# Load order, V of the first tiles, eviction engines and a split last tile in a gated attention and feed-forward kernel

## The chip, the cores and the metric

The kernel runs on one core of a Trainium2 chip. The metric is the device time of one execution in microseconds (us), measured over several executions. The profile's "span", from the first to the last instruction, is about 2 us shorter than that time. Engines are named as in the profile: PE (TensorE matmul), PEld (its weight loads), DVE (VectorE), ACT (ScalarE), POOL (GpSimd), SP (SyncE, which only issues DMA here).

On a single core "slow" cannot mean that one die is slower than the other. It means a run over 1.5% above the fastest of its kernel.

## The reference

```python
x = A_x                                              # 2048 x 512, bf16
g = sigmoid((x * gate_w).sum(-1))
# A: linear attention, 32 heads of 16
q, k, v = split(x @ wqkv)
pq, pk  = q @ w_phi[h], k @ w_phi[h]                 # per head, 16 x 16
phi     = concat(softmax(p), softmax(-p))            # for q and k
num, den = phi_q @ (phi_k^T v),  phi_q @ sum(phi_k)
a = (num / den) @ wo
# B: two-layer perceptron, 1376 hidden
b = relu(x @ w1) @ w2
out = g * a + (1 - g) * b
```

## The kernel before

The program is one list of operations per engine; each waits for named events. PE's order is what matters most. It multiplies `x` by W1 in "units" (`hunit`: 4 matmuls of 128x512, then a Relu on ScalarE); there are 4 column groups of 512 rows of x, with 11 units each. It folds `w_phi` into the Q and K weights (`pre`), which needs those weights transposed; then it runs 16 attention tiles of 128 rows (`atile`), with the units of groups 1 and 2 between them, then the units of group 3, then 16 output tiles.

The loads, in their order of issue (cuts marked `...`):

```python
for j in range(4):                     # x rows 0..511, two tiles each on SP's and ScalarE's queue
    p.dma(("sp", "act")[j // 2], ... out=XS[:, j, :], in_=x2[...], ev=f"x0{j}")
w1cuts = [0, 256, 512, 1024, DFF]      # four pieces of W1 on ScalarE's and SP's queues
for i in range(4):
    p.dma(("act", "act", "sp", "sp")[i], ... out=W1[:, :, a:b], ... ev=f"w1{i}")
p.dma("pool", ... out=WPS ...)         # w_phi, then four tiny loads of gate_w
...
p.wait("pool", ["x01", "x03"])
p.wait("sp", ["x03"])
p.dma("pool", ... out=WV ...)                                    # V's weight, 512 KB
p.dma("sp", ... dma_start_transpose(out=WQKT, in_=A_wqkv[:, 0:2 * D]))   # Q and K weights, 1 MB
for c in range(1, NCH):                                          # x rows 512..2047, transposed
    p.dma("sp", ... dma_start_transpose(out=XT[...], in_=x2[...]))
```

One attention tile. Q and K share one pair of PSUM banks, so that the matmuls of tile m + 1 wait for the last Exp of tile m (`em`):

```python
def atile(m):
    first = xready(m // 4) + [f"em{m - 1}"]
    ...  # PE: 8 matmuls, Q and K, into banks 0 and 1
    ...  # PE: 4 matmuls, V, into bank 2, after the V copy of tile m - 1
    ...  # ScalarE: Exp(+) and Exp(-) of both banks, 128x1024 each: ep, em
    p.op("dve", ... tensor_copy(VS[:, b, :, 0:64], PS[:, 2, :] ...), ev=f"cv{m}")       # V copy
    p.op("dve", ... tensor_reduce(ZB[:, b, 64:128], ...), after=[f"em{m}"])             # sums for K
    p.op("dve", ... reciprocal(SC[:, b, 64:128], ...))
    p.op("dve", ... tensor_reduce(ZB[:, b, 0:64], ...))                                 # sums for Q
    p.op("dve", ... reciprocal(SC[:, b, 32:64], ...))
    p.op("dve", ... tensor_tensor(SC[:, b, 0:32], ..., ALU.mult), ev=f"sc{m}")          # small product
    p.op("pool", ... K scaled ...);  p.op("pool", ... Q scaled ...)
    p.dma("sp", ... dma_start_transpose(out=PHQ[...], in_=FM[:, b, 0, :]))
```

The order on PE:

```python
for kt in range(8): hunit(0, kt)
pre()                                     # needs the transposed Q and K weights
for kt in range(8, KT): hunit(0, kt)
for m in range(NT):
    atile(m)
    want = (m + 1) * len(mid) // NT       # 22 units over 16 tiles
    while done < want: hunit(*mid[done]); done += 1
    if m >= LAG: kv(m - LAG)
...  # late units, kvfin(), gate(), finB(0), nd(0), nd(1), finB(1), nd(2), finA(0), comb(0), finA(1), comb(1)
for m in range(2, NT):
    if m + 1 < NT: nd(m + 1)              # PHI of Q times KV; VectorE divides, DMA transposes to OT
    finB(m); finA(m); comb(m)             # W2 product, WO product (ScalarE scales), VectorE combines
```

The softmax here doesn't subtract the row's maximum and nothing guards it: scores larger than these inputs give would overflow.

## Time and profile before

Three timed runs took 168.22 to 170.77 us, median 168.73. The profile shown first is of a slow execution (172.73 us, span 170.9).

From the page of the kernel before: busy tenths of the engines, the granted PE clock and the DMA rate in 40 slices of 4.3 us each.

```profile
PE   6469369999999999989999999897999999999991
DVE  3500032199999999999999994155453355434531
PEclk9969956999999999999999999999999999999999
GB/s 137 259 155 104 150 225 166 186 267 62 61 61 65 63 61 63 61 47 80 61 61 61 37 89 61 1 31 83 74 84 69 88 69 63 92 67 90 61 83 40
```

Up to slice 7 PE has gaps and a low clock; from slice 9 to 24 VectorE is at 9; after that PE alone is full. The gaps of the start are named by the chain of waits (start us, length us, what):

```profile
4.83 18.19 DMA PHQ<-in_A_wqkv_dram
...
23.06 3.59 PE PS L253 x32
26.65 3.67 PE PS L223 x12
30.32 1.74 PE PS L273 x8
```

The transposing load of the Q and K weights (`PHQ` lends its space) takes 18.2 us, then come the products of `pre` (L253), three units (L223) and the first QK tile (L273). While that load is under way, the DMA rate collapses. The stretches are of the same profile; their last number is GB/s, the one before the DMA share, and before that stands the clock:

```profile
4.00:8.00 4.00, 1.84 (x18) 1.18 (x16) 2.16 (x8) 0.00 (x0) 1.25 (x2) 1.00 0.90 244
12.00:16.00 4.00, 2.90 (x14) 1.37 (x15) 0.00 (x0) 1.46 (x4) 0.00 (x0) 1.00 1.25 88
16.00:20.00 4.00, 2.45 (x12) 0.90 (x10) 0.00 (x0) 2.29 (x4) 0.00 (x0) 1.00 1.18 94
22.00:26.00 4.00, 2.94 (x28) 2.94 (x29) 1.97 (x3) 1.36 (x3) 0.00 (x0) 0.50 1.18 234
```

Plain loads alone (4 to 8 us) move 244 GB/s, transposes alone (22 to 26 us) 234, the two together about 90, with the DMA engines shown as busy throughout.

A stretch of the tiles shows what VectorE (the third busy time, 42.96 of 44 us) is doing there:

```profile
38.00:82.00 44.00, 43.05 (x256) 20.26 (x256) 42.96 (x61) 28.01 (x36) 30.14 (x21) 1.00 0.32 61
```

| stage (span of the slow profile) | us | what fills it |
|---|---|---|
| start to the first QK tile | 0 to 30.2 | weight load; PE at half clock after waiting |
| tiles, first QK to last QK | 30.2 to 93.4 | 4.22 us per tile on PE; VectorE 98% busy |
| last tile and late units | 93.4 to 109.4 | PE |
| output | 109.4 to 170.9 | PE, 3.5 us per tile |

### The profile page before, as it was taken

Reading aid. Unit: us, or ns where it says so; the run is one execution under the profiler, and the core shown is the slowest. Engines: PE = TensorE matmul, PEld = TensorE weight load, DVE = VectorE, ACT = ScalarE, POOL = GpSimd, SP = SyncE. Lnnn points to the kernel's source line nnn. Section 1 sums busy time; section 2 is a strip of 40 time slices with the busy share of each in tenths; the row PEclk is TensorE's granted clock in tenths of the full one; section 3 lists DMA queues with packets and bytes.
Section 4 is the critical chain, followed back from the end, with each engine's and each line's share of the span. In section 5 each row is a group of like instructions: output and inputs, shape, how many; then the busy total and the mean of one; then the engine's idle time right before and its main releaser. Section 6 shows DMA issues by size and latency. Waiting matters only on the chain.

```text
span 170.9 us, 2373 instructions
## 1 busy us (share of the span) xinstructions
PE 153.3 (90%) x919; PEld 73.3 (43%) x919; DVE 104.2 (61%) x174; ACT 73.3 (43%) x102; POOL 54.6 (32%) x48
## 2 busy tenths in 40 slices
PE   6469369999999999989999999897999999999991
PEld 2314065434444445444434454353445544454440
DVE  3500032199999999999999994155453355434531
ACT  3024325886657577575566666403111311122111
POOL 8200000456666666666666664000000000000000
PEclk9969956999999999999999999999999999999999
DMA  4999998672225222253222332013232332324231
GB/s 137 259 155 104 150 225 166 186 267 62 61 61 65 63 61 63 61 47 80 61 61 61 37 89 61 1 31 83 74 84 69 88 69 63 92 67 90 61 83 40
DMA packets 42378, 15.57 MB, mean 91 GB/s; under 512 B 37136, under 2 KB 41760, under 8 KB 42368
## 3 DMA queue, kind: packets, MB, share of 16 engines
q1 hardware_dynamic: 40192, 12.17, 37.3%
q0 software_dynamic: 832, 2.48, 4.9%
q10 hardware_dynamic: 1344, 0.79, 1.7%
q8 instruction: 7, 0.11, 0.3%
q14 instruction: 3, 0.02, 0.0%
HBM read 4.41 MB, written 2.10 MB: 38 GB/s over the span
## 4 chain that ended last, share of the span: by engine, by line
PE 44%; DVE 32%; DMA 14%; issue 6%; ACT 2%; ACTq 0%; DVEq 0%
PE PS L384 21%; DMA PHQ<-in_A_wqkv_dram 11%; DVE ZB L294 9%; DVE ZB L299 9%; PE PS L223 9%; PE PS L394 8%; DVE VS L291 5%; DVE SC L302 3%; DMA OT<-in_A_x_dram 2%; PE PS L253 2%; PE PS L360 2%; DVE SC L297 2%; DVE SC L304 2%; DMA OT<-OTM 1%; ACT FM L288 1%
## 5 line engine op out<-in xcount | busy, mean ns | idle before, releaser
L223 PE MATMUL PS<-XT,W 128*128 128x512 bf16 (+1 forms) x176 | 44.3, 397 | 3.8 <-DVE Wbd L200 2.2
L384 PE MATMUL PS<-W,HT 128*128 128x512 bf16 (+1 forms) x176 | 40.6, 379 | 0.9 <-ACT EG L347 0.8
L288 ACT ACTIVATE FM<-PS 128x1024 bf16<-128x1024 f32 x32 | 31.0, 1021 | 20.6 <-PE PS L273 20.6
L307 POOL TENSOR_TENSOR FM<-FM,SC 128x1024 bf16<-128x1024 bf16 x16 | 30.8, 1927 | 22.9 <-DVE SC L297 22.9
L237 ACT ACTIVATE HT<-PS 128x512 bf16<-128x512 f32 (+1 forms) x44 | 26.2, 598 | 16.9 <-PE PS L223 16.8
L399 ACT ACTIVATE TFA<-PS,GT 128x512 bf16<-128x512 f32 x16 | 11.0, 687 | 47.5 <-PE PS L394 47.5
L223 PEld LDWEIGHTS PS<-XT,W 128*128 128x128 bf16 (+1 forms) x176 | 17.9, 104 | 25.5 <-issue 2.9
L405 DVE SCALAR_TENSOR_TENSOR OSB<-PS,OMG,TFA 128x512 bf16<-128x512 f32 x16 | 12.0, 751 | 27.6 <-ACT TFA L399 27.6
L273 PE MATMUL PS<-WqP,XT 128*128 128x512 bf16 x64 | 24.3, 380 | 1.0 <-ACT FM L288 0.6
L273 PE MATMUL PS<-WkP,XT 128*128 128x512 bf16 x64 | 24.2, 379 | 0.0
L384 PEld LDWEIGHTS PS<-W,HT 128*128 128x128 bf16 (+1 forms) x176 | 16.2, 97 | 18.7 <-issue 1.2
L294 DVE TENSOR_REDUCE ZB<-FM 128x64 f32<-128x1024 bf16 x16 | 19.3, 1204 | 0.4 <-ACT FM L288 0.4
L299 DVE TENSOR_REDUCE ZB<-FM 128x64 f32<-128x1024 bf16 x16 | 18.6, 1161 | 0.0
L311 POOL TENSOR_TENSOR FM<-FM,SC 128x512 bf16<-128x512 bf16 x16 | 16.9, 1055 | 2.0
L279 PE MATMUL PS<-WV,XT 128*128 128x512 bf16 x64 | 16.5, 380 | 1.1 <-DVE VS L291 0.9
L394 PE MATMUL PS<-WO,OT 128*128 128x512 bf16 x64 | 16.4, 378 | 1.0 <-DMA OT<-OTM 1.0
L291 DVE CAST VS<-PS 128x512 bf16<-128x512 f32 x16 | 10.9, 679 | 6.0 <-PE PS L279 6.0
L370 DVE TENSOR_TENSOR OTM<-PS,RDEN 128x512 bf16<-128x512 f32 x16 | 11.1, 692 | 0.5
L258 DVE CAST WqP<-PS 128x512 bf16<-128x512 f32 x2 | 1.4, 691 | 15.6 <-PE PS L253 15.6
L279 PEld LDWEIGHTS PS<-WV,XT 128*128 128x128 bf16 x64 | 5.8, 98 | 10.0 <-DVE VS L291 3.8
L273 PEld LDWEIGHTS PS<-WqP,XT 128*128 128x128 bf16 x64 | 6.2, 97 | 8.6 <-ACT FM L288 2.5
L394 PEld LDWEIGHTS PS<-WO,OT 128*128 128x128 bf16 x64 | 6.1, 97 | 8.8 <-issue 0.9
(48 smaller groups left out, 94.7 us busy)
## 6 DMA issues: line engine op xcount, KB each, us to landing
out_dram<-OSB SPq DMA_DIRECT2D x16, 128.0 KB, 1.7
W<-in_B_w_dram POOLq DMA_DIRECT2D x1, 1280.0 KB, 6.6
W<-in_B_w_dram ACTq DMA_DIRECT2D x2, 256.0 KB, 8.6
W<-in_B_w_dram SPq DMA_DIRECT2D x1, 512.0 KB, 6.9
WV<-in_A_wqkv_dram POOLq DMA_DIRECT2D x1, 512.0 KB, 14.6
WO<-in_A_wo_dram POOLq DMA_DIRECT2D x1, 512.0 KB, 6.8
W<-in_B_w_dram SPq DMA_DIRECT2D x1, 352.0 KB, 10.8
OT<-in_A_x_dram ACTq DMA_DIRECT2D x2, 128.0 KB, 3.0
```

The costliest lines, as they stand in the source:

```text
L223: p.op("pe", lambda e, c=c, kt=kt, M=M, dt=dt, bank=bank: e.matmul(PS[0:M, bank, :], W1[:, dt, kt * P:kt * P + M], XT[:, dt, c * 512:(c + ...
L237: p.op("act", lambda e, c=c, kt=kt, Mr=Mr, bank=bank: e.activation(HT[0:Mr, kt, c * 512:(c + 1) * 512], PS[0:Mr, bank, :], ACT.Relu), afte ...
L273: p.op("pe", lambda e, m=m, dt=dt, which=which, W=W: e.matmul(PS[:, which, :], XT[:, dt, m * P:(m + 1) * P], W[:, dt, :], start=(dt == 0), ...
L279: p.op("pe", lambda e, m=m, dt=dt: e.matmul(PS[:, 2, :], XT[:, dt, m * P:(m + 1) * P], WV[:, dt, :], start=(dt == 0), stop=(dt == NDT - 1) ...
L288: p.op("act", lambda e, o=fm5[:, :, :, s, :], i=src, s=s: e.activation(o, i, ACT.Exp, scale=(1.0 if s == 0 else -1.0)), after=[f"qk{m}"] + ...
L291: p.op("dve", lambda e, b=b: e.tensor_copy(VS[:, b, :, 0:64], PS[:, 2, :].rearrange("p (g c) -> p g c", g=NG)), after=[f"v{m}"] + ([f"kv{m ...
L294: p.op("dve", lambda e, b=b: e.tensor_reduce(ZB[:, b, 64:128], FM[:, b, 1, :].rearrange("p (g f) -> p g f", f=DH), AX.X, ALU.add), after=[ ...
L299: p.op("dve", lambda e, b=b: e.tensor_reduce(ZB[:, b, 0:64], FM[:, b, 0, :].rearrange("p (g f) -> p g f", f=DH), AX.X, ALU.add), ev=f"zq{m}")
L307: p.op("pool", lambda e, b=b, fk=fk: e.tensor_tensor(fk, fk, SC[:, b, 64:128].unsqueeze(2).to_broadcast([P, 2 * H, DH]), ALU.mult), after= ...
L311: p.op("pool", lambda e, b=b, fq=fq: e.tensor_tensor(fq, fq, SC[:, b, 0:32].unsqueeze(2).to_broadcast([P, H, DH]), ALU.mult), after=[f"sc{ ...
L384: p.op("pe", lambda e, kt=kt, M=M, m=m, bank=bank: e.matmul(PS[:, bank, :], HT[0:M, kt, m * P:(m + 1) * P], W2[0:M, kt, :], start=(kt == 0 ...
L394: p.op("pe", lambda e, t=t, m=m, bank=bank: e.matmul(PS[:, bank, :], OT[:, t, m * P:(m + 1) * P], WO[:, t, :], start=(t == 0), stop=(t == ...
```

## The change

Its intent: no transposing transfer overlaps a plain one; PE does V of the first tiles where it used to wait for the weights (the "filler"); VectorE is relieved of the V copy (to ScalarE) and of the small product (to GpSimd); the last output tile is cut in two halves so that its evictions overlap matmuls. The diff, cut to its core:

```diff
+        w1cuts = [0, 384, 896, DFF]
+        for j in range(4): p.dma("sp", ... out=XS[:, j, :] ...)      # x, all on SP's queue
+        load_w1(0) ... load_w1(1); load_w1(2)                        # W1 now on GpSimd's queue
+        p.dma("pool", ... out=WV ...);  p.dma("pool", ... out=WPS ...)
         for dt in range(NDT):
-            p.dma("pool", ... W1[:, dt, DFF:DFF + 1], in_=gate_w ...)
+            p.dma("sp", ... W1[:, dt, DFF:DFF + 1], in_=gate_w ...)
-        p.wait("pool", ["x01", "x03"])
-        p.wait("sp", ["x03"])
+        p.wait("sp", ["w12", "wv"])
         p.dma("sp", ... dma_start_transpose(out=WQKT ...))
...
-                p.dma("sp", ... out=GL ...)                          # gate logits
+                p.dma("act", ... out=GL ...)
...      # atile: V matmuls and V copy move out, into vtile(m)
-            p.op("dve", ... tensor_tensor(SC[:, b, 0:32] ...), ev=f"sc{m}")
+            p.op("pool", ... tensor_tensor(SC[:, b, 0:32] ...), ev=f"sc{m}")
+        def vtile(m): ...            # V copy: VectorE for m < 4, ScalarE for the others
...
-        for kt in range(8): hunit(0, kt)
-        pre()
-        for kt in range(8, KT): hunit(0, kt)
+        for kt in range(KT): hunit(0, kt)
+        vtile(0); vtile(1); pre(0); vtile(2); pre(1); vtile(3)
         for m in range(NT):
             atile(m)
-            want = (m + 1) * len(mid) // NT
+            if m >= 4: vtile(m)
+            want = 2 * (m + 1) if m < 4 else 8 + (m - 3) * (len(mid) - 8) // (NT - 4)
...
+        last(NT - 1)     # W2 product of columns 0..255, WO product, W2 product of columns 256..511
```

Not shown: ScalarE takes two of the four copies of x's transposes out of PSUM, and VectorE builds its masks after the other two instead of before them.

More of the change, by code (lines that the diff above doesn't have):

```diff
@@ L133, in bass_gated_mix__linear_kernel_hedgehog__dense_activation_relu__prompt_kernel, with load_w1 @@
         p = _Plan(["sp", "pool", "act", "dve", "pe"])
+        w1cuts = [0, 384, 896, DFF]
+        def load_w1(i):
+            a, b = w1cuts[i], w1cuts[i + 1]
+            p.dma("pool", lambda e, a=a, b=b: e.dma_start(
+                out=W1[:, :, a:b], in_=B_w1[:, a:b].rearrange("(j p) n -> p j n", p=P)), f"w1{i}", ev=f"w1{i}")
         p.op("dve", lambda e: e.memset(WARM[:, :], 1.0), ev="warm")
+        for j in range(4):
+            p.dma("sp", lambda e, j=j: e.dma_start(out=XS[:, j, :], in_=x2[j * P:(j + 1) * P, :]),
+                  f"x0{j}", ev=f"x0{j}")
+        load_w1(0)
         p.op("pool", lambda e: e.iota(COLI[:, :], [[1, P]], channel_multiplier=0))
         p.op("pool", lambda e: e.iota(ROWI[:, :], [[0, P]], channel_multiplier=1), ev="iota0")
+        load_w1(1)
+        load_w1(2)
+        p.dma("pool", lambda e: e.dma_start(
+            out=WV[:, :, :], in_=A_wqkv[:, 2 * D:3 * D].rearrange("(j p) n -> p j n", p=P)), "wv", ev="wv")
+        p.dma("pool", lambda e: e.dma_start(
+            out=WPS[:, :, :], in_=A_w_phi.rearrange("(g hl) r c -> (hl r) g c", g=NDT)), "wps", ev="wps")
         p.op("pool", lambda e: e.iota(COL16[:, :], [[1, 8], [0, 16]], channel_multiplier=0), ev="iota1")
@@ L141, in bass_gated_mix__linear_kernel_hedgehog__dense_activation_relu__prompt_kernel @@
              after=["iota0"], ev="idn")
-        p.op("dve", lambda e: e.tensor_single_scalar(ROW16[:, :], ROWI[:, :], 4, ALU.arith_shift_right), ev="r16")
-        p.op("dve", lambda e: e.tensor_single_scalar(ROW32[:, :], ROWI[:, :], 5, ALU.arith_shift_right), ev="r32")
-        p.op("dve", lambda e: e.tensor_tensor(M16[:, :], ROW16[:, :], COL16[:, :], ALU.is_equal),
-             after=["iota1", "r16"], ev="m16")
-        p.op("dve", lambda e: e.tensor_tensor(M32[:, :], ROW32[:, 0:64], COL16[:, 0:64], ALU.is_equal),
-             after=["r32"], ev="m32")
-        for b in range(NB):
-            p.op("dve", lambda e, b=b: e.memset(VS[:, b, :, 64:65], 1.0), ev=f"one{b}")
-        for j in range(4):
-            p.dma(("sp", "act")[j // 2], lambda e, j=j: e.dma_start(out=XS[:, j, :], in_=x2[j * P:(j + 1) * P, :]),
-                  f"x0{j}", ev=f"x0{j}")
-        w1cuts = [0, 256, 512, 1024, DFF]
-        for i in range(4):
-            a, b = w1cuts[i], w1cuts[i + 1]
-            p.dma(("act", "act", "sp", "sp")[i], lambda e, a=a, b=b: e.dma_start(
-                out=W1[:, :, a:b], in_=B_w1[:, a:b].rearrange("(j p) n -> p j n", p=P)), f"w1{i}", ev=f"w1{i}")
-        p.dma("pool", lambda e: e.dma_start(
-            out=WPS[:, :, :], in_=A_w_phi.rearrange("(g hl) r c -> (hl r) g c", g=NDT)), "wps", ev="wps")
         for dt in range(NDT):
-            p.dma("pool", lambda e, dt=dt: e.dma_start(
+            p.dma("sp", lambda e, dt=dt: e.dma_start(
                 out=W1[:, dt, DFF:DFF + 1], in_=gate_w[dt * P:(dt + 1) * P].rearrange("(p o) -> p o", o=1)),
                 "gw", ev=f"gw{dt}")
-        p.wait("pool", ["x01", "x03"])
-        p.wait("sp", ["x03"])
-        p.dma("pool", lambda e: e.dma_start(
-            out=WV[:, :, :], in_=A_wqkv[:, 2 * D:3 * D].rearrange("(j p) n -> p j n", p=P)), "wv", ev="wv")
+        p.wait("sp", ["w12", "wv"])
         p.dma("sp", lambda e: e.dma_start_transpose(out=WQKT, in_=A_wqkv[:, 0:2 * D]), "wqk", ev="wqk")
@@ L196, in bass_gated_mix__linear_kernel_hedgehog__dense_activation_relu__prompt_kernel @@
             dst = XT[:, :, j * P:(j + 1) * P]
-            p.op("dve", lambda e, s=src, d=dst: e.tensor_copy(d, s), after=[f"xt{j}"], ev=f"xc{j}")
+            if j % 2 == 0:
+                p.op("dve", lambda e, s=src, d=dst: e.tensor_copy(d, s), after=[f"xt{j}"], ev=f"xc{j}")
+            else:
+                p.op("act", lambda e, s=src, d=dst: e.activation(d, s, ACT.Copy), after=[f"xt{j}"], ev=f"xc{j}")
+        p.op("dve", lambda e: e.tensor_single_scalar(ROW16[:, :], ROWI[:, :], 4, ALU.arith_shift_right), ev="r16")
+        p.op("dve", lambda e: e.tensor_single_scalar(ROW32[:, :], ROWI[:, :], 5, ALU.arith_shift_right), ev="r32")
+        p.op("dve", lambda e: e.tensor_tensor(M16[:, :], ROW16[:, :], COL16[:, :], ALU.is_equal),
+             after=["iota1", "r16"], ev="m16")
+        p.op("dve", lambda e: e.tensor_tensor(M32[:, :], ROW32[:, 0:64], COL16[:, 0:64], ALU.is_equal),
+             after=["r32"], ev="m32")
+        for b in range(NB):
+            p.op("dve", lambda e, b=b: e.memset(VS[:, b, :, 64:65], 1.0), ev=f"one{b}")
         for gt in range(NDT):
@@ L215, in hunit @@
             M = P if kt < KT - 1 else KREM + 1
-            w1s = [i for i in range(4) if w1cuts[i] <= kt * P < w1cuts[i + 1]][0]
+            w1s = [i for i in range(3) if w1cuts[i] <= kt * P < w1cuts[i + 1]][0]
             after = xready(c) + [f"w1{w1s}"]
@@ L232, in hunit @@
                     after=[f"h{u}"], ev=f"gr{c}")
-                p.dma("sp", lambda e, c=c: e.dma_start(
+                p.dma("act", lambda e, c=c: e.dma_start(
                     out=GL[:, c * 4:(c + 1) * 4],
@@ L239, in hunit, with pre @@
                 after=[f"h{u}"], ev=f"rl{u}")
-        def pre():
-            PB = [0, 1, 2, 6, 7]
-            for i in range(8):
+        def pre(half):
+            PB = [0, 1, 6, 7]
+            for i in range(4 * half, 4 * half + 4):
                 which, dt = i // 4, i % 4
-                bank = PB[i % 5]
+                bank = PB[i % 4]
                 dst = (WqP, WkP)[which]
                 after = ["wqk"] + [f"wbd{g}" for g in range(NDT)]
-                if i < 4:
-                    after.append(f"xc{i}")
-                if i >= 5:
-                    after.append(f"pc{i - 5}")
+                if i == 0:
+                    after.append("cv1")
+                if i >= 4:
+                    after.append(f"pc{i - 4}")
                 for gt in range(NDT):
@@ L277, in atile @@
                         ev=(f"qk{m}" if dt == NDT - 1 and which == 1 else None))
-            for dt in range(NDT):
-                p.op("pe", lambda e, m=m, dt=dt: e.matmul(
-                    PS[:, 2, :], XT[:, dt, m * P:(m + 1) * P], WV[:, dt, :],
-                    start=(dt == 0), stop=(dt == NDT - 1)),
-                    after=((["wv"] + ([f"cv{m - 1}"] if m else [])) if dt == 0 else ()),
-                    ev=(f"v{m}" if dt == NDT - 1 else None))
             fm5 = FM[:, b, :, :].rearrange("p a (h s f) -> p a h s f", h=H, s=2)
@@ L290, in atile @@
                     after=[f"qk{m}"] + free, ev=f"{nm}{m}")
-            p.op("dve", lambda e, b=b: e.tensor_copy(
-                VS[:, b, :, 0:64], PS[:, 2, :].rearrange("p (g c) -> p g c", g=NG)),
-                after=[f"v{m}"] + ([f"kv{m - NB}"] if m >= NB else []), ev=f"cv{m}")
             p.op("dve", lambda e, b=b: e.tensor_reduce(
@@ L299, in atile @@
             p.op("dve", lambda e, b=b: e.tensor_reduce(
-                ZB[:, b, 0:64], FM[:, b, 0, :].rearrange("p (g f) -> p g f", f=DH), AX.X, ALU.add), ev=f"zq{m}")
+                ZB[:, b, 0:64], FM[:, b, 0, :].rearrange("p (g f) -> p g f", f=DH), AX.X, ALU.add),
+                after=([f"sc{m - NB}"] if m >= NB else []), ev=f"zq{m}")
             zq = ZB[:, b, 0:64].rearrange("p (h s) -> p h s", s=2)
             p.op("dve", lambda e, b=b, zq=zq: e.reciprocal(SC[:, b, 32:64], zq[:, :, 1]),
-                 after=[f"zq{m}"] + ([f"pq{m - NB}"] if m >= NB else []), ev=f"rq{m}")
-            p.op("dve", lambda e, b=b, zq=zq: e.tensor_tensor(SC[:, b, 0:32], zq[:, :, 0], SC[:, b, 32:64], ALU.mult),
-                 after=[f"rq{m}"], ev=f"sc{m}")
+                 after=[f"zq{m}"] + ([f"sc{m - NB}"] if m >= NB else []), ev=f"rq{m}")
             fk = FM[:, b, 1, :].rearrange("p (g f) -> p g f", f=DH)
@@ L309, in atile @@
                 after=[f"rz{m}"], ev=f"pk{m}")
+            p.op("pool", lambda e, b=b, zq=zq: e.tensor_tensor(SC[:, b, 0:32], zq[:, :, 0], SC[:, b, 32:64], ALU.mult),
+                 after=[f"rq{m}"], ev=f"sc{m}")
             fq = FM[:, b, 0, :].rearrange("p (h s f) -> p h s f", h=H, s=2)[:, :, 1, :]
@@ L316, in atile, with vtile @@
                 f"tq{b}", after=[f"pq{m}"] + ([f"pm7"] if m == 12 else []), ev=f"tq{m}")
+        def vtile(m):
+            b = m % NB
+            bank = 0 if m == 1 else 2
+            prev = {0: [], 1: [], 2: ["cv0"]}.get(m, [f"cv{m - 1}"])
+            for dt in range(NDT):
+                p.op("pe", lambda e, m=m, dt=dt, bank=bank: e.matmul(
+                    PS[:, bank, :], XT[:, dt, m * P:(m + 1) * P], WV[:, dt, :],
+                    start=(dt == 0), stop=(dt == NDT - 1)),
+                    after=((xready(m // 4) + ["wv"] + prev) if dt == 0 else ()),
+                    ev=(f"v{m}" if dt == NDT - 1 else None))
+            dst, src = VS[:, b, :, 0:64], PS[:, bank, :].rearrange("p (g c) -> p g c", g=NG)
+            after = [f"v{m}"] + ([f"kv{m - NB}"] if m >= NB else [])
+            if m < 4:
+                p.op("dve", lambda e, d=dst, s=src: e.tensor_copy(d, s), after=after, ev=f"cv{m}")
+            else:
+                p.op("act", lambda e, d=dst, s=src: e.activation(d, s, ACT.Copy), after=after, ev=f"cv{m}")
         def kv(m):
@@ L410, in comb, with last @@
                 out=o2[m * P:(m + 1) * P, :], in_=OSB[:, ob, :]), f"out{ob}", after=[f"cb{m}"], ev=f"out{m}")
-        for kt in range(8):
-            hunit(0, kt)
-        pre()
-        for kt in range(8, KT):
-            hunit(0, kt)
+        def last(m):
+            ob = m % 3
+            for hf in range(2):
+                if hf == 1:
+                    finA(m)
+                bank = (5 - m % 2, 0)[hf]
+                cs = slice(hf * 256, hf * 256 + 256)
+                after = [f"cb{m - 2}", f"om{m - 1}"]
+                for kt in range(KT):
+                    M = P if kt < KT - 1 else KREM
+                    p.op("pe", lambda e, kt=kt, M=M, bank=bank, cs=cs: e.matmul(
+                        PS[:, bank, 0:256], HT[0:M, kt, m * P:(m + 1) * P], W2[0:M, kt, cs],
+                        start=(kt == 0), stop=(kt == KT - 1)),
+                        after=(after if kt == 0 else ()), ev=(f"fb{m}{hf}" if kt == KT - 1 else None))
+            for hf in range(2):
+                bank = (5 - m % 2, 0)[hf]
+                cs = slice(hf * 256, hf * 256 + 256)
+                p.op("dve", lambda e, bank=bank, cs=cs: e.scalar_tensor_tensor(
+                    out=OSB[:, ob, cs], in0=PS[:, bank, 0:256], scalar=OMG[:, m:m + 1],
+                    in1=TFA[:, m % 2, cs], op0=ALU.mult, op1=ALU.add),
+                    after=[f"fb{m}{hf}", f"ta{m}", f"out{m - 3}"], ev=f"cb{m}{hf}")
+                p.dma("sp", lambda e, cs=cs: e.dma_start(
+                    out=o2[m * P:(m + 1) * P, cs], in_=OSB[:, ob, cs]), f"last{hf}",
+                    after=[f"cb{m}{hf}"], ev=f"last{hf}")
+        for kt in range(KT):
+            hunit(0, kt)
+        vtile(0)
+        vtile(1)
+        pre(0)
+        vtile(2)
+        pre(1)
+        vtile(3)
         mid = [(c, kt) for c in (1, 2) for kt in [KT - 1] + list(range(KT - 1))]
@@ L422, in bass_gated_mix__linear_kernel_hedgehog__dense_activation_relu__prompt_kernel @@
             atile(m)
-            want = (m + 1) * len(mid) // NT
+            if m >= 4:
+                vtile(m)
+            want = 2 * (m + 1) if m < 4 else 8 + (m - 3) * (len(mid) - 8) // (NT - 4)
             while done < want:
@@ L444, in bass_gated_mix__linear_kernel_hedgehog__dense_activation_relu__prompt_kernel @@
         comb(1)
-        for m in range(2, NT):
-            if m + 1 < NT:
-                nd(m + 1)
+        for m in range(2, NT - 1):
+            nd(m + 1)
             finB(m)
@@ L450, in bass_gated_mix__linear_kernel_hedgehog__dense_activation_relu__prompt_kernel @@
             comb(m)
-        p.wait("sp", [f"out{m}" for m in range(NT - 3, NT)])
+        last(NT - 1)
+        p.wait("sp", [f"out{m}" for m in range(NT - 3, NT - 1)] + ["last0", "last1"])
         sems = {}
```

## The prediction

> **What bounds the kernel now** (timeline, chain of waits, windows).
>
> 1. Start, 0 to 30.2 us. The transposing load of the Q and K weights is issued at 4.83 us and lands 18.2 us later, while plain loads of W1 and V's weight share the DMA engines. In 12 to 20 us the DMA moved only 63 to 113 GB/s, against 240 to 260 for plain loads alone (2 to 8 us) and 220 to 264 for transposes alone (20 to 28 us). PE runs 8 of the 11 first units, waits 4.6 us for the weights, and comes back at half clock (granted 0.50 from 22 to 28 us). The first QK tile starts at 30.15.
> 2. Sixteen tiles, to 98.4 us. VectorE's work comes back every 4.37 us (V copy 0.68, reductions 1.20 and 1.16, reciprocals 0.55 and 0.35, product 0.55), 98% busy. PE needs about 4.0 us per tile (a 128x512 matmul every 0.2155 us).
> 3. Eleven late units, to 109.4 us, PE bound.
> 4. Sixteen output tiles at 3.5 us, PE bound, and a tail: ScalarE 0.69, VectorE 0.75, store about 2.
>
> **What the change does.**
>
> Start: plain loads first. 2.43 MB at about 255 GB/s is 9.5 us, landed by about 12 us. Then the transposing load of 1 MB runs alone: 2.4 us of issue per 0.5 MB (as the x transposes) plus 2 us to land, so it lands at about 19. Meanwhile PE has all 11 units and V of two tiles (13 x 0.86 us from about 6.5 us, plus up to 1.7 while the clock is low), so it arrives at 18 to 19.5, with almost no wait, and warm. The Trainium skill ("TensorE: Matmul & The Clock Gate", Part 1) says idleness of about 3.4 us halves the clock; the 0.50 after the 4.6 us wait agrees. With weight products, eight evictions (0.69 VectorE, 0.60 ScalarE) and V of tile 2 in between, QK tile 0 starts at about 23.4, with four V tiles (3.4 us of PE) already done.
>
> Tiles: VectorE loses V copy and product and needs about 3.3 us. The next limit is the round trip of the single QK PSUM pair: matmuls 1.72, exps 1.94, latencies 0.3; unobstructed it took 3.94 us (34.07 to 38.01). ScalarE carries exps 1.94, V copy about 0.65, one or two Relus of 0.60, just fitting. GpSimd: 1.93 + 1.06[...]. PE: 3.7 in tiles with one unit; 4.55 in two tiles with two. So about 4.0 us instead of 4.37, 5 to 6 us over the stage; late units start at about 88 instead of 98.4.
>
> Output: unchanged per tile. Splitting the last tile hides the scaling behind matmuls: 0.9 us less.
>
> Sum: start and tiles 10.4, end 0.9: 11 us off the profiled execution (172.7, a slow run). The fast timed runs are at 168.2 to 168.7; part of those 4 us is probably variation of that same weight load, not available twice. So I take 9: 159.5 us.
>
> **What would show it.** Weight transpose landing in about 7 us after an issue near 12; first QK tile at 22 to 25; tile period 3.9 to 4.1, released by ScalarE's exps; VectorE about 80% in the tiles; late units at about 88; V copy on ScalarE 0.6 to 0.7.
>
> **What would make it wrong.** GpSimd's queue slower than 255 GB/s, so the transposes start at 15; no gain from keeping transfers apart; ScalarE delaying exps (V copy, two Relus, four DMA issues) to 4.3 us per tile; a smaller gain as before's fast runs already have a quicker load.
>
> Range 155.5 to 163.5. Faster by over 2%: 0.96; within 2%: 0.03; slower: 0.01.

## The result, and the profile after

The changed kernel took 162.44 us (median of 4 runs, 162.36 to 163.23); the kernel before took 169.24 in the same rounds. The ratio is 0.963 (95% interval 0.956 to 0.970). It is the mean time of one kernel's fast runs over that of the other's of the same rounds, so not quite the ratio of these medians. The time lies inside the stated range, 2.9 us above the point.

The same lines of the page, for the changed kernel (span 160.1, a fast run; a slice is 4.0 us):

```profile
PE   6699799899999999999999998979999999999983
DVE  1401391788888878687888521544455544445532
PEclk9999999999999999999999999999999999999999
GB/s 126 259 234 186 242 185 87 359 150 66 66 70 66 66 70 66 70 68 66 66 66 70 66 66 0 0 98 92 74 68 66 70 98 66 72 92 70 66 67 64
```

The clock never drops, VectorE has fallen to 8 or 7 in most slices of the tiles, and the DMA rate of the start has no hole. Its chain of waits no longer shows the weight load, but PE's own work (L228 units, L320 V, L258 the products of `pre`, L278 QK, L287 the Exps):

```profile
7.25 9.66 PE PS L228 x44
16.91 1.74 PE PS L320 x8
...
18.68 0.70 DVE VS L328
...
19.51 1.05 PE PS L258 x16
...
23.41 1.91 PE PS L278 x8
...
25.35 1.94 ACT FM L287 x2
```

The same kind of stretches, clock, DMA share and GB/s last (the long one is of the tiles, with VectorE at 35.16 of 44 us):

```profile
4.00:8.00 4.00, 2.58 (x22) 1.63 (x21) 1.70 (x11) 1.19 (x2) 1.94 (x4) 1.00 0.85 259
8.00:10.00 2.00, 2.00 (x11) 0.88 (x9) 0.00 (x0) 1.19 (x2) 0.00 (x0) 1.00 1.03 400
12.00:16.00 4.00, 4.00 (x20) 1.91 (x19) 0.51 (x3) 2.76 (x5) 0.00 (x0) 1.00 0.85 185
16.00:20.00 4.00, 3.12 (x22) 1.56 (x21) 1.45 (x3) 1.78 (x3) 0.00 (x0) 1.00 1.18 242
38.00:82.00 44.00, 43.20 (x269) 20.88 (x268) 35.16 (x45) 33.08 (x47) 35.09 (x34) 1.00 0.30 66
```

The transposing load is issued at 11.49 us and lands 6.5 us later (last number, from the list of DMA issues):

```profile
PHQ<-in_A_wqkv_dram SPq DMA_TRANSPOSE x1, 6.5
```

But the PE chain reaches `pre` only at 19.5, 1.5 us after that landing: by then the weight load no longer bounds the start.

A slow profile of before and a fast one of after must not be subtracted. The first experiment therefore was a fast profile of the kernel before.

### The profile page after: what moved, and what is told of

Read it like the earlier page. It is cut to its first block, busy times and chain, and to the rows that moved or that the text cites. A ratio compares the mean times of both kernels' runs of the same rounds, so it can differ in the third digit from the quotient of the medians.

```text
span 160.1 us, 2385 instructions
## 1 busy us (share of the span) xinstructions
PE 149.4 (93%) x930; PEld 72.6 (45%) x930; DVE 89.0 (56%) x145; ACT 78.7 (49%) x116; POOL 58.2 (36%) x63
## 4 chain that ended last, share of the span: by engine, by line
PE 66%; ACT 20%; DVE 5%; DMA 3%; issue 3%; ACTq 1%; DVEq 0%
PE PS L398 19%; ACT FM L287 17%; PE PS L278 17%; PE PS L228 14%; PE PS L408 8%; DMA OT<-OTM 3%; PE PS L320 3%; PE PS L178 2%; PE PS L374 2%; ACT TFA L413 1%; DVE VS L328 1%; DVE OTM L384 1%; PE PS L340 1%; DVE WkP L263 1%; ACT GROW L234 1%
## 5 line engine op out<-in xcount | busy, mean ns | idle before, releaser
L228 PE MATMUL PS<-XT,W 128*128 128x512 bf16 (+1 forms) x176 | 41.3, 379 | 0.7 <-DVE VS L202 0.7
L398 PE MATMUL PS<-W,HT 128*128 128x512 bf16 (+1 forms) x165 | 38.1, 379 | 0.9 <-ACT EG L361 0.8
L287 ACT ACTIVATE FM<-PS 128x1024 bf16<-128x1024 f32 x32 | 31.0, 1020 | 15.7 <-PE PS L278 15.7
L242 ACT ACTIVATE HT<-PS 128x512 bf16<-128x512 f32 (+1 forms) x44 | 25.6, 604 | 8.1 <-PE PS L228 5.8
L290 DVE TENSOR_REDUCE ZB<-FM 128x64 f32<-128x1024 bf16 x16 | 19.5, 1220 | 14.2 <-ACT FM L287 14.2
L228 PEld LDWEIGHTS PS<-XT,W 128*128 128x128 bf16 (+1 forms) x176 | 17.3, 100 | 20.5 <-DVE VS L202 0.9
L278 PE MATMUL PS<-WqP,XT 128*128 128x512 bf16 x64 | 24.4, 381 | 2.1 <-ACT FM L287 1.3
L419 DVE SCALAR_TENSOR_TENSOR OSB<-PS,OMG,TFA 128x512 bf16<-128x512 f32 x15 | 11.3, 751 | 25.2 <-ACT TFA L413 25.2
L278 PE MATMUL PS<-WkP,XT 128*128 128x512 bf16 x64 | 24.3, 379 | 0.0
L398 PEld LDWEIGHTS PS<-W,HT 128*128 128x128 bf16 (+1 forms) x165 | 15.1, 97 | 17.4 <-issue 1.2
L295 DVE TENSOR_REDUCE ZB<-FM 128x64 f32<-128x1024 bf16 x16 | 18.6, 1161 | 0.0
L320 PE MATMUL PS<-WV,XT 128*128 128x512 bf16 x64 | 16.3, 379 | 0.0
L278 PEld LDWEIGHTS PS<-WqP,XT 128*128 128x128 bf16 x64 | 6.2, 97 | 11.0 <-ACT FM L287 4.5
L320 PEld LDWEIGHTS PS<-WV,XT 128*128 128x128 bf16 x64 | 6.1, 98 | 7.1
L293 DVE RECIPROCAL SC<-ZB 128x64 f32<-128x64 f32 x16 | 8.8, 553 | 0.5
L278 PEld LDWEIGHTS PS<-WkP,XT 128*128 128x128 bf16 x64 | 6.3, 98 | 5.7
```

What stands on the lines that cost most here:

```text
L228: p.op("pe", lambda e, c=c, kt=kt, M=M, dt=dt, bank=bank: e.matmul(PS[0:M, bank, :], W1[:, dt, kt * P:kt * P + M], XT[:, dt, c * 512:(c + ...
L242: p.op("act", lambda e, c=c, kt=kt, Mr=Mr, bank=bank: e.activation(HT[0:Mr, kt, c * 512:(c + 1) * 512], PS[0:Mr, bank, :], ACT.Relu), afte ...
L278: p.op("pe", lambda e, m=m, dt=dt, which=which, W=W: e.matmul(PS[:, which, :], XT[:, dt, m * P:(m + 1) * P], W[:, dt, :], start=(dt == 0), ...
L287: p.op("act", lambda e, o=fm5[:, :, :, s, :], i=src, s=s: e.activation(o, i, ACT.Exp, scale=(1.0 if s == 0 else -1.0)), after=[f"qk{m}"] + ...
L290: p.op("dve", lambda e, b=b: e.tensor_reduce(ZB[:, b, 64:128], FM[:, b, 1, :].rearrange("p (g f) -> p g f", f=DH), AX.X, ALU.add), after=[ ...
L295: p.op("dve", lambda e, b=b: e.tensor_reduce(ZB[:, b, 0:64], FM[:, b, 0, :].rearrange("p (g f) -> p g f", f=DH), AX.X, ALU.add), after=([f ...
```

## The experiments

"Changed kernel" below always means the one after the change. The kernel before varied between the batches (medians 169.2 to 171.4) and within them; the changed kernel was timed in one batch alone. Every run gave correct results.

### b_again: the kernel before once more

> The kernel before, unchanged, for a profile in the fast state (the one shown first was 172.7 us, slow). Theory: the kernel before varies (168.2 to 170.8) because its Q/K weight load, mixed with plain loads, lands at a varying time; then a fast profile has a span near 166.5 and its first QK tile starts 3 to 4 us before 30.15, with the tiles again at 4.37 us and the output stage again 3.5 us per tile. Rival: the slow profile was slow everywhere (tiles over 4.37 us in it); then the first QK tile again starts near 30 and the tiles are shorter than 4.37 us.

170.56 us (169.43 to 173.56); the profiled run, a fast one, has a span of 168.2. The weights landed at 22.65 us, against 23.0 in the slow profile: no difference to speak of. So the theory's cause does not explain these two profiles. (It isn't ruled out for other runs: in the profile of b_act, below, whose start is that of the kernel before, the weights landed at 21.02.) The first QK tile nevertheless starts at 27.30 instead of 30.15. Chain of waits of the fast run:

```profile
4.42 18.23 DMA PHQ<-in_A_wqkv_dram
...
22.70 2.18 PE PS L253 x32
24.88 2.59 PE PS L223 x12
27.47 1.74 PE PS L273 x8
```

Compare 2.18 and 2.59 with 3.59 and 3.67 of the slow one: the same 32 + 12 matmuls at full and at half clock, together 2.5 us. In the slow run PE had finished its eight units early and idled 4.6 us before the weights came; in the fast one W1 came later, PE was still busy at 21 us and waited 1.5 us. So what makes the slow profile slower than the fast one is mostly a cold PE clock after a wait, 2.5 of 2.7 us. That other slow runs have the same cause is not shown: by their mean clocks, slow runs of the kernel before (0.956 to 0.990) and fast ones (0.957 to 1.000) can't be told apart. The Trainium skill, "TensorE: Matmul & The Clock Gate", Part 1, says that the clock falls to half after an idle window of about 3.4 us, and that the window runs free, so the moment varies from run to run; 4.6 us idle (0.50 granted) and 1.5 us idle (1.00) agree. But the traces show no sharp limit at 3.4: 2.2 us idle before the first unit of the slow profile and 2.6 us in b_act were also followed by half clock (0.50 from 8.2 to 11.6 and from 15.1 to 18.6 us), 1.8 us in the fast profile was not. Tiles (63.3 us from first to last QK) and output (61.6) are the same in both.

Stages of the two fast profiles, before (b_again) and after, in us of span:

| stage | before | after | gain |
|---|---|---|---|
| to the first QK tile | 27.30 | 23.41 | 3.9 |
| first to last QK tile | 63.31 | 59.95 | 3.4 |
| last QK tile to first output matmul | 16.01 | 15.81 | 0.2 |
| output | 61.55 | 60.98 | 0.6 |
| span | 168.17 | 160.15 | 8.0 |

The times of the same rounds differ by less, 6.8 us (169.24 to 162.44): the profiled run of b_again took 169.99, and time minus span is 1.8 us for it and 2.2 for the changed kernel.

### b_sep: only keeping the transfers apart

```diff
-        p.wait("sp", ["x03"])
+        p.wait("sp", ["x01", "x03", "w10", "w11", "w12", "w13", "wv"])   # ahead of the first transpose
```

> The kernel before, with one change: the transposing loads wait until x, W1 and V's weight have landed (no V filler, no other queue, no offload). Theory (keeping the two kinds of transfer apart is what brings the weights early): issue near 11 to 12 us, landing 6.5 us later, near 18 (not 23), QK tile 0 near 24 to 25, tiles still 4.37 us; 163 to 165 us. Rival (mixing costs nothing, the bytes just queue): the weights land at 22 or later and the time is the same as before or longer, 168 to 171.

166.58 us (165.82 to 167.95), ratio to before 0.980 (0.969 to 0.991). Issue at 12.9, landing 6.6 us later, at 19.5; first QK tile at 25.34, 2.0 us earlier than in the fast profile before; tiles unchanged. The mechanism holds, but the gain is smaller than 3 to 5 us, because something else then ends last:

```profile
1.67 9.09 DMA W<-in_B_w_dram
...
10.89 10.02 PE PS L223 x32
20.91 2.00 PE PS L253 x32
```

W1's first piece lands only at 10.8 us, with all the other loads under way beside it; PE starts cold at 10.9, takes 10 us for eight units and is itself the last to be ready. In the changed kernel W1 comes piece after piece through one queue, its first piece lands at 5.9, and PE starts at 7.25.

### a_mix, a_mix2, a_mix3: the changed kernel, without its wait

a_mix takes away only the wait:

```diff
-        p.wait("sp", ["w12", "wv"])
```

> The changed kernel, with one part undone: the transposing loads do not wait for the plain ones, so they are issued near 4.5 us and overlap them. Theory: the Q/K weights then land no earlier than in the changed kernel (17.9 us) and W1 and V's weight land late, so that PE stalls in the first units or before V of tile 0; 2 to 5 us slower than the changed kernel, 164.5 to 167.5. Rival (order alone is what matters, overlap is harmless as PE has filler): 162 to 163, within 1 us of the changed kernel.

162.48 us (162.38 to 162.63), the same as the changed kernel; the rival held. The transposing load was issued at 4.5 and landed at 15.2, earlier than with the wait (18.0). The first QK tile is at 23.57. So the added wait gains nothing. Why did the overlap not hurt? Between 6 and 10 us the trace's DMA packet records show only 29 transposing packets, beside 342 GB/s of plain data: the transposes stood behind. One candidate was the four gate_w loads ahead of them in SP's queue. a_mix2 moves these to ScalarE's queue:

```diff
             p.dma("sp" -> "act", ... W1[:, dt, DFF:DFF + 1], in_=gate_w ...)
-        p.wait("sp", ["w12", "wv"])
```

> The changed kernel without the wait for the plain loads (as a_mix), and with the four gate_w loads (512 packets of 2 or 4 bytes) moved from SP's queue to ScalarE's, so that nothing stands before the transposing loads in SP's queue. In a_mix the transposes moved nothing before 10 us of span, and nothing was lost. Theory (real mixing costs: in the kernel before, 256 B transposing packets that took 18 ns alone took up to about 330 ns while plain packets ran): now the transposes do mix with W1 and V loads, total DMA rate falls below 150 GB/s for some 4 us, W1 or V land later than 11.4, and PE stalls; 163.5 to 167 us. Rival (mixing with 4 KB packets from GpSimd's queue is harmless, it was the 512 and 1024 B packets of the hardware queues, or the late V load, that mixed badly): 162 to 163, Q/K weights landing by 15 to 16.

173.02 us (170.57 to 174.39, two fast runs and two slow ones), far above the 163.5 to 167 expected: its fast runs, 170.57 and 172.47, are 8 to 10 us above a_mix, and slower than the kernel before (ratio 1.017, 1.005 to 1.029). The profile is of a slow run (171.4 us of span). The transposes are now issued at 2.6 us, ahead of two of the W1 pieces and of V's weight. W1's second piece lands 15.6 us after its issue and V's weight 16.8, the first QK tile starts at 34.68, and the hole is back, from 16 to 20 us (windows of a_mix2, GB/s last):

```profile
4.00:8.00 4.00, 2.70 (x18) 1.63 (x16) 1.21 (x5) 0.66 (x2) 1.92 (x4) 1.00 1.18 230
8.00:12.00 4.00, 3.37 (x9) 1.17 (x10) 0.50 (x7) 1.13 (x2) 0.00 (x0) 1.00 0.92 183
12.00:16.00 4.00, 1.87 (x5) 0.44 (x3) 0.00 (x0) 1.19 (x2) 0.00 (x0) 1.00 1.22 211
16.00:20.00 4.00, 1.61 (x4) 0.59 (x5) 0.00 (x0) 0.00 (x0) 0.00 (x0) 0.64 1.26 72
```

The chain of waits has `2.66 15.60 DMA W<-in_B_w_dram`, then PE's units. Mixing can thus be costly with the large packets of GpSimd's queue too. The DMA packet records (256-byte packets are the transposing ones):

```
run, us of span        transposing packets  median  over 100 ns   all traffic
after,  14 to 18 alone        3956           18 ns      1%          253 GB/s
before, 12 to 20 mixed        1552           18 ns     34%           91 GB/s
b_again, 12 to 20 mixed       2166           18 ns     20%          101 GB/s
a_mix2, 14 to 20 mixed        1022           19 ns     42%           94 GB/s
```

Not every mixed stretch is slow: from 10 to 14 us of a_mix2, 535 transposing packets ran beside plain ones, and the DMA moved 269 GB/s, 235 of it plain. Why the rate then falls was not found.

Two things had changed in a_mix2, the packets ahead and the moment of issue. a_mix3 separates them: gate_w stays on ScalarE's queue, and SP waits for the third x tile first.

```diff
-        p.wait("sp", ["w12", "wv"])
+        p.wait("sp", ["x02"])
```

> As a_mix2 (gate_w loads on ScalarE's queue, transposes not held back until the plain loads have landed), but SP first waits for the third x tile, so the transposes are issued near 4.5 us as in a_mix, when all plain loads have been issued. This tells apart why a_mix was fast and a_mix2 slow. Queue theory (in a_mix the 512 tiny gate_w packets stood before the transposes in SP's queue and kept them out until the plain loads were nearly done): without them the transposes mix again, W1 or V or the Q/K weights land late, 165 us or more. Timing theory (issuing them 2 us later, behind the plain loads, is enough): 162 to 163.5, Q/K weights near 15.

165.93 us (165.27 to 166.59), which is the number of the queue theory, but not by its cause. The transposes were issued at 5.1, after the last large plain load (V's weight, issued 4.2 to 4.9), landed at 15.5, and V's weight landed at 11.8, like in a_mix: nothing mixed for long. The time was lost elsewhere: the last x tile landed at 7.7 us (chain of waits: `2.13 5.60 DMA OT<-in_A_x_dram`), units started at 8.91 instead of 7.25 and took 10.96 us instead of 9.66 for a half clock at first; together the 2.95 us by which the first QK tile is later (26.36). The gate_w loads on ScalarE's queue, issued from 0.8 us on, probably held x up; that was not tried by itself. So for the weights the timing theory holds: it is enough to issue the transposes behind the plain loads.

### b_vfirst: the kernel before, with V's weight issued earlier

```diff
-        p.wait("pool", ["x01", "x03"])
-        p.wait("sp", ["x03"])
-        p.dma("pool", ... out=WV ...)          # issued at 5.0 us, after the transposing load (4.4)
+        p.wait("sp", ["x01", "x03"])
+        p.dma("pool", ... out=WV ...)          # first on GpSimd's queue, 1.4 us
```

> The kernel before with the V weight load issued first of GpSimd's loads, near 1.4 us instead of 5.0, so that all plain loads are issued ahead of the transposing load (near 4.4); no wait for their landing is added, and W1 stays in pieces on SP's and ScalarE's queues. Order theory (a_mix and a_mix3 escaped the mixing because every plain load had been issued before the transposes): the Q/K weights land near 15 to 17 instead of 22.7, first QK tile at 24 to 25.5, 165 to 167 us. Rival (W1 in 512 and 1024 B packets on the hardware queues mixes whatever the order): the Q/K weights land at 20 or later, 168 us or more.

166.67 us (166.13 to 167.79), ratio 0.982 (0.971 to 0.992), the gain of b_sep without any added wait. The transposing load, issued at 4.8, landed at 16.7 instead of 22.65, although W1 still comes in small packets on the hardware queues; the first QK tile is at 25.22. The order theory held. (The edit also makes SP wait for one more x tile, which moves the issue from 4.4 to 4.8; the slow profile of before has its issue at 4.83 too, and landed at 23.0.) As in b_sep, W1's first piece (10.9 us) and PE's cold clock then set the start. In the kernel before, one 512 KB load issued 0.6 us too late was what mixed with the transposes. Its packet records agree: from 12 to 20 us of the slow profile the only large plain packets are V's, of 4,096 bytes; from 8 to 10 us, with W1's packets of 512 and 704 bytes and only 20 of V's beside 342 transposing ones, the DMA moved 276 GB/s. Whether V's weight would mix as badly from another queue was not tried.

### b_act and a_dve: the two offloads

b_act is the kernel before with the V copy on ScalarE and the small product on GpSimd:

```diff
-            p.op("dve", ... tensor_copy(VS[:, b, :, 0:64], PS[:, 2, :] ...)
+            p.op("act", ... activation(VS[:, b, :, 0:64], PS[:, 2, :] ..., ACT.Copy)
-            p.op("dve", ... tensor_tensor(SC[:, b, 0:32] ...)
+            p.op("pool", ... tensor_tensor(SC[:, b, 0:32] ...)      # after the K scaling
```

> The kernel before, with one change: the V copy of all tiles runs on ScalarE and the small product on GpSimd. The start is untouched. Theory (VectorE's 4.37 us bound the tiles, the QK round trip of 3.94 is next): tiles at 3.95 to 4.1 us, first QK tile where the kernel before has it, 163 to 165 us, 4 to 6 us less than before. Rival (the tiles were PE bound anyway, or ScalarE takes over the bound): tiles stay above 4.25 us and the time falls by under 2 us.

169.74 us (167.34 to 172.28, two fast runs and two slow ones), ratio 0.988 (0.971 to 1.005): unclear as a time. The profile (a fast run) is clear: first to last QK tile 61.95 us instead of 63.31, 1.4 us less where 4 to 6 were expected. The tile period went from 4.22 to 4.13. (Its first QK tile also starts 1.1 us earlier than in b_again, at 26.17; that is the earlier landing of the weights, which the edit doesn't touch.) I had read 4.22 nowhere; I had taken VectorE's 4.37 for the period. On PE, the distances between the first QK matmuls of successive tiles in the kernel before are 3.93, 3.93, 4.32, 3.92, 3.94, 4.57, 3.92, 4.65, 3.92, 3.95, 5.24, 4.00, 3.92, 5.18, 3.92 us. Most tiles run at the QK round trip, 3.92; those with two units overflow to 4.3 to 4.6; only two, over 5, have the overflow and a wait for VectorE too (0.9 us of waits of the V matmuls for the V copy in all; from b_again's list of waits, us in total, times, longest):

```profile
PE PS L279 <- DVE VS L291: 0.9, 2, 0.5
```

VectorE comes back every 4.37 us because it falls behind PE by about 0.15 us a tile; it is nearly always busy, but stalls PE only when it is a whole tile behind. With the offloads the two long tiles shrink to 4.58 and 4.57, and the others hardly change.

a_dve undoes both offloads in tiles 4 to 15 of the changed kernel (the copy on VectorE, ahead of the sums; the product after the reciprocal).

> The changed kernel with both offloads undone for tiles 4 to 15: V copy (ahead of the reductions, as before had it) and small product on VectorE. VectorE then needs 4.37 us in these tiles, PE and ScalarE 3.94. Theory (VectorE lags and only stalls PE once it is a whole tile behind, as in the kernel before, where 2 of 15 tiles were longer for it): 1 to 3 us slower than the changed kernel, 163.4 to 165.4, the stalls in the last tiles. Rival of the prediction (VectorE's 4.37 sets every tile): 12 times 0.43, 5 us slower, 167 to 168.

164.49 us (164.16 to 164.67), 2.0 us slower than the changed kernel, as the theory said. First to last QK tile 61.66 instead of 59.95. The tenth distance grew from 4.58 to 5.17, and the last three are 4.30, 4.37 and 4.36 (3.91 to 3.93 before the edit): only there VectorE, which falls behind from tile 4 on, sets the pace. From the waits between 70 and 86 us:

```profile
PE PS L321 <- DVE VS L329: 1.4, 3, 0.5
```

So the offloads are worth about 2 us in the changed kernel and 1.4 in the old one; that PE's shorter tiles make the difference is likely, but not shown.

### a_nofill: V of the first tiles

The changed kernel with `vtile(0)` to `vtile(3)` back in their tiles, all V copies on ScalarE, and `want = (m + 1) * len(mid) // NT` as before.

> The changed kernel with V of tiles 0 to 3 back in their tiles (copied by ScalarE as the others) and the 22 middle units spread evenly again. Theory (PE simply has the work earlier or later: weights land at 18, so QK tile 0 starts near 21.4 instead of 23.4, and the tiles come every 4.13 us as in b_act instead of 4.00): QK tile 15 starts near 83.4 as in the changed kernel, and the time is within 0.8 us of it, 161.8 to 163.2. Rival (the filler saves its 3.4 us of PE work, as it runs where PE would wait): QK tile 15 near 85.5 or later, 164.5 to 166.

162.86 us (161.86 to 164.24). Without the filler `pre` starts at 17.60 instead of 19.51 and the first QK tile at 21.01 instead of 23.41, 2.4 us earlier. The tiles then take 62.25 us instead of 59.95, 2.3 us more, as five of the 15 distances again are 4.3 to 4.6. The last QK tile starts at 83.26 (changed kernel: 83.36), and the spans are 160.0 and 160.1. The filler gains nothing in these profiles: since the weights land at 18, PE has little wait left to fill, and V only moves from one place to another. The four runs fall in two pairs, 161.9 and 164.0; the profiled one is of the faster. Why the other pair is slower is open: one of them has a mean clock of 0.988, which a half clock at the start would explain, the other 1.000; they have no traces. All four runs of the changed kernel lie within 0.9 us, so a steadier start thanks to the filler isn't ruled out.

### a_nosplit: the last tile whole

```diff
-        last(NT - 1)
+        finB(NT - 1); finA(NT - 1); comb(NT - 1)
```

> The changed kernel with the last output tile whole again. Theory: the split hides ScalarE's scaling and half of the combine (0.69 + 0.35) but PE waits about 0.55 us more for the last transposed tile, since the half of the W2 product before it is 1.2 us shorter; net 0.5 to 0.7, so 162.9 to 163.2, last matmul to end 3.7 instead of 2.55 us, and last matmul 0.5 us earlier. Rival (the full 0.9 us predicted): 163.3 or more.

163.97 us (162.94 to 164.79). The profiled run lost 1.9 us at the start, with a half clock in its first units (0.50 from 8 to 10 us), which has nothing to do with the edit. Its output stage takes 61.81 us, against 60.98: the split gives 0.8 us, between the theory's 0.5 to 0.7 and the rival's 0.9. From the last matmul to the end it is 3.75 us instead of 2.61, 1.1 less with the split, of which 0.3 is given back: PE waits for the last transposed tile (`OT<-OTM`), since only half of the W2 product lies before it. End of the chain of the changed kernel:

```profile
152.05 0.70 DVE OTM L384
...
152.77 2.49 DMA OT<-OTM
...
155.30 1.05 PE PS L408 x4
156.35 0.03 issue
156.38 0.69 ACT TFA L413
```

The fastest runs differ by 0.6 us (162.94 and 162.36), so the size stays open between 0.6 and 0.8.

### a_spread and a_best: using what the traces show

The tiles of the changed kernel are bound by the round trip of the QK banks (matmuls 1.72, Exps 1.94, and what lies between). PE has about 0.25 us to spare in a one-unit tile (3.93 less 1.72 + 0.86 + 0.86 + 0.25), which is too little for another unit of 0.86, but enough for one matmul of 0.2155. a_spread issues the units matmul by matmul:

```diff
+        steps = (None for u in mid + late for _ in hunit(*u))     # hunit yields after each matmul
+        quota = [10, 10, 10, 9] + [5] * 12                        # matmuls per tile
         for m in range(NT):
             ...
-            while done < want: hunit(*mid[done]); done += 1
+            for _ in range(quota[m]): next(steps)
```

> The changed kernel with the 33 units of the last three column groups issued matmul by matmul, 10, 10, 10, 9 and then 5 per tile, instead of whole units; 11 matmuls more than before fall into the tiles, as many fewer after them. Theory (in the changed kernel the QK round trip of 3.93 us bounds the tiles, PE has 0.25 us per one-unit tile to spare, and a tile with two units overflows by 0.65): all tiles 3.92 to 4.1, QK tile 15 near 82.6, last unit ended near 95.3 instead of 98.4; 159 to 160 us. Rival (tiles are bound by PE): tiles get longer by the matmuls added, same time, 162 to 163.

159.53 us (158.71 to 160.30). Eleven more matmuls lie in the tiles, and these still come every 3.955 us (4.00 in the changed kernel), the longest 4.07. The last unit ended at 94.76 instead of 98.39. PE did not bound the tiles.

a_best adds to this the other waits that the traces show.

```diff
+            p.dma(("sp", "act")[j % 2], ... out=XS[:, j, :] ...)   # x from two queues
+        warm(2)                                                    # after the x transposes
+        ... kv(NT - 1); kvfin(); 4 steps; nd(0); 8 steps; nd(1); finB(0); gate(); finA(0)
+        finB(0) waits for rl41, nd(1) for rl42, finB(1) for rl43   # each for its own bank's Relu only
+        if m == NT - 3: nd(NT - 1) ahead of comb(m)                # last division ahead of a combine
```

> a_spread and what the traces showed besides: x loads from two queues and two more warm-up matmuls (first unit near 6.6, at full clock); first two PHI products ahead of the last units and the first output tile waiting only for the Relus it needs (PE waited 0.8 + 0.85 + 0.2 us there); last PHI product's evictions ahead of the combine of tile 13 (PE waited 0.4 to 0.55 us for the last transposed tile). Estimate 159.5 less 0.6, 1.8 and 0.5: 156 to 157.5 us. If a wait merely moves, it stays at 158 to 160.

155.79 us (155.62 to 156.16), ratio to before 0.921 (0.914 to 0.928), span 153.7: a little below the estimate. It beats both kernels. Its parts were not tried one by one. Most of its step over a_spread (span 157.5 to 153.7) lies from the last unit on: from there to the end it takes 58.4 us instead of 62.7. The changed kernel there waits 0.8 us for ScalarE, and then for the first transposed tile:

```profile
99.17 2.54 PE PS L398 x11
101.70 0.27 PE PS L374 x8
...
102.00 0.37 DVE RDEN L380
...
102.39 0.69 DVE OTM L384
...
103.11 2.48 DMA OT<-OTM
...
105.72 1.04 PE PS L408 x4
```

In a_best the first PHI product (L378) lies ahead of the last units (L231), and PE goes through:

```profile
93.14 0.42 PE PS L378 x8
93.56 1.73 PE PS L231 x8
95.28 0.33 PE PS L378 x8
95.61 2.38 PE PS L402 x11
97.99 0.87 PE PS L412 x4
```

The x loads on two queues hardly helped: units start at 7.17 instead of 7.25.

## Why the prediction was right or wrong

The time, 162.44, lies in the range, and nearly every landmark is where it was put: the weight load about 6.5 us long after an issue near 12 (11.49), first QK tile at 23.4 (23.41), PE warm, tiles at 4.00 us, VectorE at 80% (35.2 of 44 us in the middle of the tiles), V copy 0.60 us on ScalarE, late units at 88 (88.35). Four steps were wrong or badly sized.

1. **"part of those 4 us is probably variation of that same weight load, not available twice. So I take 9".** The weights landed at 23.0 in the slow profile and at 22.65 in the fast one; what varied between these two was PE's clock after its wait (b_act's 21.02 shows that the landing varies as well). Either way it is a matter of the kernel before alone. The estimate of the kernel after was built up from its own parts and needed no discount. Without it, it would have been 161.4. The remaining 1.0 us is 0.1 by the start of the late units (98.63 to 88.35 in the chains, where 10.4 less was predicted), 0.4 from the output stage (61.49 in the slow profile, 60.98 after, where 0.9 less was predicted), 0.4 because time minus span is 2.2 us after and 1.8 before, and 0.1 because the profiled run is the fastest of the four.
2. **"VectorE's work comes back every 4.37 us ... 98% busy", taken as the bound of the tiles.** PE's tiles came every 4.22 us, most of them every 3.92. The offloads alone brought 1.4 us (b_act) of "5 to 6 us over the stage". The stage as a whole lost 3.4 us, but 2.3 of it by thinning out the two-unit tiles, with V moved ahead. The sum escaped this error by luck: its 10.4 us is the difference of two landmarks (98.4 and 88), which leaves 3.65 us for the tiles beside 6.75 for the start, and not the "5 to 6" of the text.
3. **"with four V tiles (3.4 us of PE) already done", as part of the gain.** a_nofill shows 2.4 us of later start against 2.3 us of shorter tiles. What made the start shorter was the load order and PE's earlier start (step 4).
4. **"Start: plain loads first ... Then the transposing load of 1 MB runs alone".** Order and separation are right as the cause (b_sep, b_vfirst, a_mix2), but the explicit wait is not needed (a_mix): issuing the plain loads first suffices. Part of the start's gain, which the prediction did not separate, is that W1's first piece comes early through one queue: with the mixing cured alone (b_sep, b_vfirst), PE still starts at about 11 us and at half clock. The profiles give its size: the first QK tile starts at 27.30 before, at 25.2 to 25.3 with the mixing cured alone, and at 21.01 in a_nofill, which has the whole new start without the filler. So about 2 us fall to the mixing and a further 4.2 to the rest of the new start, of which the filler takes 2.4 back. Which part of that rest matters (GpSimd's queue, the new cuts of W1, x on one queue, the moved copies) was not isolated.

The split was predicted at 0.9 us; the output stage shows 0.8 against a_nosplit and 0.6 against before, the times 0.6.

## What to carry to other kernels

Issue all plain loads before the first transposing one when the two can meet: one 512 KB load issued 0.6 us late cost 2 us of the start here, and three late loads 8 to 10 us of time; no wait is needed for it (a_mix, b_vfirst). An engine that is 98% busy at its own period may just be lagging: read the distance between the same instruction in successive tiles on the engine that must not wait, before calling the other one the bound. Where a loop is bound by a round trip, its slack takes work only in pieces that fit, so that a unit of four matmuls issued one at a time can be free where the whole unit is not. And when a profile of before is of a slow run, find what was slow before discounting anything for it.

## What the Trainium skill lacked or had wrong

- "DMA: Bandwidth & Descriptors", Rules for kernel authors, says of transposes from several queues: "A transpose next to ordinary DMAs needs nothing". All runs here were correct, so this agrees; but no page gives the cost in time. In the worst mixed stretches (12 to 20 us of the kernel before, 14 to 20 of a_mix2) the DMA moved 72 to 94 GB/s instead of 234 to 259 for either alone, and 34 to 42% of the transposing packets took over 100 ns instead of 1%.
- "Advanced Engine Details and Errata", X-Bar Transpose (TRN2), says "TRN2 transpose DMAs are as fast as regular DMAs". Alone, transposes here moved 234 to 253 GB/s (272 from 12 to 16 us of a_mix). That holds against the plain loads in packets of up to 1 KB (244 GB/s, 4 to 8 us of the kernel before), and not against the 400 of the best stretch (8 to 10 us of the changed kernel, GpSimd's packets of 4 KB and more).
- "DMA: Bandwidth & Descriptors", same section, says that spreading DMAs over the issuing engines doesn't help bandwidth. That agrees: 244 GB/s with the loads on three queues (4 to 8 us of the kernel before), 400 with the large ones on GpSimd's alone. But when a piece lands did change with the new arrangement: with W1 over two queues its first piece landed at 7.9 to 10.9 us (five profiles), in one queue at 5.7 to 7.5 (nine). The pieces were cut anew as well, so this is not isolated.
- "TensorE: Matmul & The Clock Gate", Part 1, puts the ramp penalty below 1% of a typical kernel's span and advises not to fit it. That speaks of the first warm-up; the 2.5 us between the two profiles of the kernel before, 1.5% of the span, come from a second stretch at half clock, after a wait, so they do not contradict it. They only show that such a stretch can be most of the difference between two runs (2.5 of 2.7 us).
